# Numerators and projections joined into one step, and TensorE in program order in blocks 1 to 3, in a fused attention and two-layer expert kernel

## The chip, the cores and the metric

The kernel runs on one core of a Trainium2 chip. The metric is the device time of one execution in microseconds (us), as the median of three runs. Engines are named as in the profile: PE is TensorE (matmuls; PEld its weight loads), DVE is VectorE, ACT is ScalarE, POOL is GpSimd, SP is SyncE, which issues most transfers.

## The reference

Three stages follow each other. 2304 tokens are 4 batches of 576; there are 8 heads of 64.

```python
def phi(x):                                   # x: q or k
    proj = np.einsum('bhsd,df->bhsf', x, w_phi)          # 64 -> 128 features
    proj = proj - np.max(np.abs(proj), axis=-1, keepdims=True)
    return np.concatenate([np.exp(proj), np.exp(-proj)], axis=-1)
q_p, k_p = (phi(q), phi(k))
kv = np.einsum('bhsf,bhsd->bhfd', k_p, v)
z = np.sum(k_p, axis=2)
num = np.einsum('bhsf,bhfd->bhsd', q_p, kv)
den = np.einsum('bhsf,bhf->bhs', q_p, z)[..., None] + 1e-06
x = num / den                                 # heads side by side: 2304 x 512
# first layer, 512 -> 1536 -> 512
g = x @ w_gate
x2 = (g * (1.0 / (1.0 + np.exp(-g))) * (x @ w_val)) @ w_out
# second layer: one of 8 experts for each token, by argmax(x2 @ gate)
out[mask] = gate_w * eom * (np.maximum(x2[mask] @ w1[e], 0.0) @ w2[e])
```

## The kernel before

**Attention** is cut into 16 units, each two heads of one batch. Units 0 to 7 are computed in a first part whose order is a table (`PLAN_TABLE`, the same in both kernels). Units 8 to 15 are written as a list of steps (`steps`), and these are what the change touches. Unit u has these steps, each with its matmuls and what empties their PSUM banks:

- `step_kv`: the sums over k features and v (L350, L359), copied out by ACT;
- `step_tq`, three times: transposes of the projected q (L381), then two exponentials on ACT;
- `step_qk(u + 1, c)`, c = 0 to 2: a third of the next unit's projection of q and k (L310), 6 matmuls into a **pair** of banks. DVE then reads the pair twice, in `qk_sub`: the maximum (L318) and the subtraction (L321). ACT makes the exponentials;
- `step_num`: for each of the two heads the numerator and denominator (`num_mm`, L401, 20 matmuls into one bank), then `normalise` on DVE (L413 to L415);
- `step_tx`, twice: transposes of the result (L420), taken by ACT and DVE into `XH` and `XL`, the input of the first layer.

The matmuls of the first layer use the whole array. Those of `step_qk` use 64 of its rows, those of `step_kv` and `step_num` 64 of its columns. A fp32 matmul of the last two kinds stands as two in the trace: 6 are x12, 20 are x40.

**The first layer** works on 6 blocks of 384 tokens, each with 12 slices f. A slice has three runs of matmuls: gate (12, L538 to L540), value (12, the same lines), and the output of the slice before (9, L576 to L578). They own banks 0 to 4. The function `pace` is called after each run, 36 times per block, and spreads over them the steps of units 8 to 15; `need[n]` says up to which step block n has to come. After each of these calls (after two of three) `fill` runs one piece of the routing of the block before: `post_log` (4 transposes, L722), `post_mm` (L730), `route_a`, `route_b` (L764, L765).

**Banks 5, 6 and 7** are shared by all these steps and pieces. `bank_no` takes the one that was used longest ago, `pair_no` the pair of neighbours that was; in a tie the lowest number. Two pairs are possible, 5 and 6, or 6 and 7, so that two thirds of a projection in a row always share bank 6. Data dependencies, through banks too, become semaphore waits on the engine that comes later.

**Order.** After the first part a scheduler puts each engine's instructions in order, by the order of the program and by what it holds to be ready. An engine runs its instructions strictly in that order.

Of the kernel before, what the change touches and what calls it, by code (L numbers as in the profile page):

```python
# [24 lines left out]
NBLK, BT = 6, 384  # L25
# [4 lines left out]
QSW = 8  # L30
# [151 lines left out]
def kernel(ctx, tc, qT, kT, v1, wphi, w1cat, wlog, mw1, mw2, consts, out):  # L182
# [86 lines left out]
    state = {"n": 0, "banks": [0, 1, 2, 3, 4, 5, 6, 7], "rd": 0}  # L269
    used = {b: 0 for b in range(8)}  # L270
# [17 lines left out]
    def rot(key, lst):  # L288
        state[key] += 1
        return lst[state[key] % len(lst)]  # L290
# [4 lines left out]
    def load_qk(u):  # L295
        SP.dma_start(out=QK[u % 2][QROWS, :], in_=qT[u])
        SP.dma_start(out=QK[u % 2][KROWS, :], in_=kT[u])
# [4 lines left out]
    def two(u):  # L302
        return u % 2 if u < PROL else 0

    def qk_mm(u, c, b):

        for j in range(3):
            t0 = (3 * c + j) * P
            for rows, w in ((QROWS, 1), (KROWS, 0)):
                PE.matmul(PS[:, b + w, j * P:(j + 1) * P], QK[u % 2][rows, t0:t0 + P], wphi_sb[rows, :],  # L310
                          start=True, stop=True)
        if c == 2 and 8 < u < 14:
            load_qk(u + 2)

    def qk_sub(u, c, b):

        ps = PS[:, b:b + 2, :BT].rearrange("p w (j f) -> p w j f", f=P)
        DVE.tensor_reduce(out=MX, in_=ps, axis=AX.X, op=ALU.max, apply_absolute_value=True)  # L318
        t = KQ[two(u)][:, 3 * c:3 * c + 3, :].rearrange("p j (w f) -> p w j f", f=P)[:, 0:3:2]
        m = MX.rearrange("p w (j o) -> p w j o", o=1).to_broadcast([P, 2, 3, P])  # L320
        DVE.tensor_tensor(out=t, in0=ps, in1=m, op=ALU.subtract)  # L321

    def k_exp(u, c):
        kq, ts_ = KQ[two(u)], slice(3 * c, 3 * c + 3)
        t = kq[:, ts_, 0:P]
        ACT.activation(kq[:, ts_, P:2 * P], t, AF.Exp, scale=-1.0)
        ACT.activation(t, t, AF.Exp)
# [48 lines left out]
    def qp(u):  # L376
        return QP[two(u)] if u < QSW else QP[2]
# [15 lines left out]
    def num_mm(u, h, b):  # L393

        kv = KV[u % 2]
        ps = PS[:, b, :325].rearrange("p (s d) -> p s d", d=65)
        for i in range(5):
            for a in range(2):
                for g in HALVES:
                    t0 = h * S + i * P + (0 if i == 4 and h == 1 else g.start)  # L400
                    PE.matmul(ps[g, i, :], qp(u)[:, a, t0:t0 + 64], kv[:, a, h * 65:h * 65 + 65], start=(a == 0),  # L401
                              stop=(a == 1), skip_group_check=True)
# [7 lines left out]
    def normalise(h, b):  # L410
        ps = PS[:, b, :325].rearrange("p (s d) -> p s d", d=65)
        rd = rot("rd", RD)[:, :5].rearrange("p (s o) -> p s o", o=1)
        DVE.tensor_scalar(out=rd, in0=ps[:, :, 64:65], scalar1=1e-6, scalar2=None, op0=ALU.add)  # L413
        DVE.reciprocal(out=rd, in_=rd)
        DVE.tensor_tensor(out=XT[:, :, h * 64:h * 64 + 64], in0=ps[:, :, 0:64], in1=rd.to_broadcast([P, 5, 64]), op=ALU.mult)  # L415
# [31 lines left out]
    steps, mark = [], {}  # L447

    def add(f, *a):
        steps.append((f, a))  # L450

    def qk(u):
        return [(step_qk, u, c) for c in range(3)] if u < 16 else []

    def warmup(n):
        for _ in range(n):
            PE.matmul(PS[:, 4, :], warm[:, 0:P], warm, start=True, stop=True)

    add(step_ov)
    for u in range(QSW, 16):  # L460
        add(step_kv, u)
        for c in range(3):
            add(step_tq, u, c)
        x = qk(u + 1)
        for s_ in x[:2]:
            add(*s_)
        add(step_num, u)
        for s_ in x[2:]:
            add(*s_)
        add(step_tx, u, 0)  # L470
        add(step_tx, u, 1)
        mark[u] = len(steps)
    pos = [0]

    def run_to(n):
        while pos[0] < min(n, len(steps)):
            f, a = steps[pos[0]]
            f(*a)
            pos[0] += 1
# [46 lines left out]
    def split(i):  # L526
        if i < len(uses):
            split_hi(i)
            split_lo(i)
# [12 lines left out]
    def mm_gv(n, f, which):  # L542
        gv_mm(n, f, which)
        split(where[n, f, which] + 3)
# [16 lines left out]
    def act_g(n, f):  # L561
        g_tanh()
        g_mul()

    def act_v(n, f):
        v_mul()
        g_hi(f)
        g_lo(f)

    def o_mm(n, f):  # L570
        i = where[n, f, 2]
        woh, wol = WH[i % 4], WL[i % 4]
        for t in range(3):
            ps = PS[:, OUTB[t], :]
            ts_ = slice(t * P, (t + 1) * P)
            PE.matmul(ps, GH[f % 2][:, ts_], woh, start=(f == 0), stop=False)  # L576
            PE.matmul(ps, GH[f % 2][:, ts_], wol, start=False, stop=False)  # L577
            PE.matmul(ps, GL[f % 2][:, ts_], woh, start=False, stop=(f == NFT - 1))  # L578

    def mm_o(n, f):  # L580
        o_mm(n, f)
        split(where[n, f, 2] + 3)
# [128 lines left out]
    def post_x2(n, t):  # L711
        i = 3 * n + t
        x2 = X2[t]
        ACT.activation(x2, PS[:, OUTB[t], :], AF.Copy, scale=0.5)
        SP.dma_start(out=x2d[i * P:(i + 1) * P, 0:DM], in_=x2)
# [181 lines left out]
    def load_w(s, part):  # L897
        e = SP.value_load(EXI[0:1, s:s + 1], min_val=0, max_val=NE - 1)
        src = (mw1 if part == 0 else mw2)[ds(e, 1)].rearrange("o p c -> (o p) c")
        kw = {}  # L900
        if s >= 2:
            kw["cond"] = SP.value_load(CHI[0:1, s:s + 1], min_val=0, max_val=1)
        SP.dma_start(out=R[s % 2][:, part * 4096:(part + 1) * 4096], in_=src, **kw)
# [7 lines left out]
    def xt(s):  # L911
        ps = PS[:, XB, :]
        for k in range(4):
            PE.transpose(ps[:, k * P:(k + 1) * P], XG[s % 4][:, k * P:(k + 1) * P], ident)
        p3 = ps.rearrange("p (k t) -> p k t", k=4)
        ACT.activation(XCH[s % 2], p3, AF.Copy)  # L916
        tt(XCL[s % 2], p3, XCH[s % 2].bitcast(F32), ALU.subtract)
# [88 lines left out]
    POOL.memset(CHI[:, 0:2], 1)  # L1006
    first_part()
    state["banks"] = [5, 6, 7]
    need = {1: mark[8] - 2, 2: mark[11], 3: mark[15], 4: 0, 5: 0}
    prev = (0, NFT - 1)  # L1010

    def post(n):
        ops = []
        for t in range(3):
            ops += [(post_log, (n, t)), (post_mm, (n, t))]
        return ops + [(route_a, (n,)), (route_b, (n,))]
# [14 lines left out]
    def fill(n):  # L1031
        while todo and n > 0:
            f, a = todo.pop(0)
            f(*a)
            n -= 1

    todo = []
    for n in range(1, NBLK):
        s0, s1 = pos[0], max(need[n], pos[0])
        for f in range(NFT):  # L1040
            def pace(g):
                run_to(s0 + ((s1 - s0) * (3 * f + g) + 35) // 36)
                if g != 2 or n == 5:
                    fill(1)
            mm_gv(n, f, 0)
            act_g(n, f)
            pace(1)
            mm_gv(n, f, 1)
            act_v(n, f)
            pace(2)  # L1050
            if prev is not None:
                mm_o(*prev)
                if prev[1] == NFT - 1:
                    for t in range(3):
                        post_x2(prev[0], t)
                    todo += post(prev[0])
                    if prev[0] == 4:
                        todo += [(totals, (EARLY_T,)), (route_early, ()), (load_w, (0, 0)),
                                 (idle, ()), (idle, ()), (early, ())]
            prev = (n, f)  # L1060
            pace(3)
            if n == 5 and f == 10:
                xt(0)
            if n == 5 and f == 10:
                load_w(1, 0)
                load_w(1, 1)
    mm_o(*prev)
    for t in range(3):
        post_x2(5, t)
# [59 lines left out]
```

## Time and profile before

| | |
|---|---|
| time, median of 3 runs | 920.05 us (918.99 to 921.12) |
| the profiled execution | 920.25 us, its span 918.5 us |
| PE busy | 894.5 us, 97% of the span |
| DVE, ACT, POOL busy | 577.0, 559.4, 393.0 us |

The span falls into a first part (to about 170 us), blocks 1 to 3 with units 8 to 15 (to about 482 us), blocks 4 and 5 (to about 650 us), and the expert layer. Matmuls overlap in the trace, each being longer than the distance to the next, so that small gaps do not show in the busy time; the starts of neighbours show them.

### The profile page before, as it was taken

What the parts mean: (1) busy time and instruction counts of PE and PEld (TensorE: products, weight loads), DVE (VectorE), ACT (ScalarE), POOL (GpSimd) and SP (SyncE); (2) the same over time, 40 slices, a digit from 0 to 9 for tenths busy, and PEclk for the clock granted to TensorE, in tenths of its full rate; (3) what the DMA queues carried; (4) which work ended last, traced back from release to release, by engine and by line L of the source; (5) the groups of instructions that cost most, each with busy time, mean ns of one, the idle gap of its engine ahead of it and who ended that gap; (6) DMA issues with size and microseconds to landing.
All of it is one profiled execution on the core that took longest, in us unless ns stands there. A gap on an engine that the chain in (4) does not pass through costs nothing. (4 is left out here: it accounts for less than half of the span.)

```text
span 918.5 us, 18395 instructions
## 1 busy us (share of the span) xinstructions
PE 894.5 (97%) x7256; PEld 784.8 (85%) x7258; DVE 577.0 (63%) x977; ACT 559.4 (61%) x975; POOL 393.0 (43%) x318
## 2 busy tenths in 40 slices
PE   8899999999999999999999999979999999999995
PEld 6789989999998998898899999969877888888884
DVE  6999776443336435445433422772699988888993
ACT  5878775544353545544444444334688899888883
POOL 1667989445543434433345566566101111112200
PEclk9999999999999999999999999999999999999998
DMA  8767543200020111110000000090001147166240
GB/s 231 221 176 216 168 143 101 62 16 1 2 76 5 38 42 27 50 42 1 2 2 35 1 1 35 2 375 39 35 24 48 47 161 284 30 224 228 64 172 10
DMA packets 20940, 78.90 MB, mean 86 GB/s; under 512 B 5358, under 2 KB 5614, under 8 KB 19056
## 3 DMA queue, kind: packets, MB, share of 16 engines
q1 hardware_dynamic: 17280, 67.60, 22.8%
q0 software_dynamic: 3200, 9.48, 3.1%
q8 instruction: 59, 0.97, 0.4%
q10 hardware_dynamic: 368, 0.59, 0.3%
q14 instruction: 33, 0.27, 0.1%
HBM read 123.23 MB, written 10.00 MB: 145 GB/s over the span
## 5 line engine op out<-in xcount | busy, mean ns | idle before, releaser
L524 POOL TENSOR_TENSOR arena_r<-arena,arena_r 128x512 fp32r<-128x512 f32 x216 | 278.7, 1294 | 246.7 <-ACT arena_r L520 239.3
L520 ACT ACTIVATE arena_r<-arena 128x512 fp32r<-128x512 f32 x216 | 136.2, 631 | 229.3 <-PE banks L539 139.7
L538 PE MATMUL banks<-arena_r 128*128 128x384 f32 x576 | 202.4, 351 | 4.2 <-DVE arena L550 4.1
L890 DVE TENSOR_TENSOR arena_r<-arena,arena_r 128x1024 fp32r<-128x1024 f32 x160 | 193.1, 1255 | 20.3 <-ACT arena_r L889 18.9
L540 PE MATMUL banks<-arena_r 128*128 128x384 f32 x576 | 194.2, 337 | 0.0
L539 PE MATMUL banks<-arena_r 128*128 128x384 f32 x576 | 193.9, 337 | 0.0
L889 ACT ACTIVATE arena_r<-arena 128x1024 fp32r<-128x1024 f32 x160 | 161.9, 1067 | 18.4 <-PE banks L924 10.9
L550 DVE SCALAR_TENSOR_TENSOR arena<-arena,banks 128x384 f32<-128x384 f32 x72 | 39.7, 552 | 130.1 <-ACT arena L547 129.8
L924 PE MATMUL banks<-arena_r 128*128 128x512 f32 x480 | 117.0, 396 | 0.0
L538 PEld LDWEIGHTS banks<-arena_r 128*128 128x128 f32 x576 | 108.6, 189 | 9.5 <-DVE arena L550 4.9
L952 POOL DMA_INDIRECT out_dram<-arena x20 | 20.7, 1037 | 218.9 <-ACT arena L951 218.9
L539 PEld LDWEIGHTS banks<-arena_r 128*128 128x128 f32 x576 | 108.9, 189 | 1.2
L540 PEld LDWEIGHTS banks<-arena_r 128*128 128x128 f32 x576 | 108.7, 189 | 0.0
L924 PEld LDWEIGHTS banks<-arena_r 128*128 128x128 f32 x480 | 88.2, 188 | 20.3 <-ACT arena_r L916 2.1
L576 PE MATMUL banks<-arena_r 128*128 128x512 f32 x216 | 87.6, 405 | 0.0
L577 PE MATMUL banks<-arena_r 128*128 128x512 f32 x216 | 85.1, 394 | 1.0 <-POOL arena_r L524 1.0
L578 PE MATMUL banks<-arena_r 128*128 128x512 f32 x216 | 84.9, 394 | 0.0
L553 DVE TENSOR_TENSOR banks<-arena,banks 128x384 f32<-128x384 f32 x72 | 40.4, 561 | 44.8 <-PE banks L540 44.1
L946 PE MATMUL banks<-arena_r 128*128 128x512 f32 x160 | 62.7, 392 | 1.0 <-ACT arena_r L889 0.7
L948 PE MATMUL banks<-arena_r 128*128 128x512 f32 x160 | 62.4, 390 | 0.0
L947 PE MATMUL banks<-arena_r 128*128 128x512 f32 x160 | 62.4, 390 | 0.0
L318 DVE TENSOR_REDUCE arena<-banks 128x6 f32<-128x768 f32 x48 | 45.8, 954 | 23.6 <-PE banks L310 22.7
(119 smaller groups left out, 1327.2 us busy)
## 6 DMA issues: line engine op xcount, KB each, us to landing
arena<-mw SPq DMA_DIRECT2D x40, 2048.0 KB
ov_conv<-w1cat SPq DMA_DIRECT2D x24, 512.0 KB
arena<-w1cat SPq DMA_DIRECT2D x12, 512.0 KB
arena<-v SPq DMA_DIRECT2D x16, 325.0 KB
x2d<-arena SPq DMA_DIRECT2D x18, 256.0 KB
arena<-qT SPq DMA_DIRECT2D x15, 288.0 KB
arena<-kT SPq DMA_DIRECT2D x15, 288.0 KB
ov_gather<-x2d,arena POOLq DMA_INDIRECT x20, 4.3
```

What stands on the lines that cost most here:

```text
L520: ACT.activation(WH[i % 4], WR[f][w], AF.Copy)
L524: POOL.tensor_tensor(out=WL[i % 4], in0=WR[f][w], in1=WH[i % 4].bitcast(F32), op=ALU.subtract)
L538: PE.matmul(ps, wh[:, c], xh, start=(k == 0), stop=False)
L539: PE.matmul(ps, wh[:, c], xl, start=False, stop=False)
L540: PE.matmul(ps, wl[:, c], xh, start=False, stop=(k == 3))
L576: PE.matmul(ps, GH[f % 2][:, ts_], woh, start=(f == 0), stop=False)
L577: PE.matmul(ps, GH[f % 2][:, ts_], wol, start=False, stop=False)
L578: PE.matmul(ps, GL[f % 2][:, ts_], woh, start=False, stop=(f == NFT - 1))
L889: ACT.activation(h, src, AF.Copy)
L890: DVE.tensor_tensor(out=l, in0=src, in1=h.bitcast(F32), op=ALU.subtract)
L924: PE.matmul(PS[:, HB[h], :], lhs, w[:, h * 512:(h + 1) * 512], start=a, stop=b)
L946: PE.matmul(ps, HTH[:, k, :], wh[:, cs], start=(k == 0), stop=False)
```

## The change

Units 8 to 15 get another list of steps. The numerator of head h and third h of the next projection are one step, `step_num_qk(u, h)`, for h = 0 and 1: the 20 and the 6 matmuls stand behind each other, then `normalise`, then `qk_sub`. Its banks are written out: bank 7 and pair 5, 6 for h = 0; bank 5 and pair 6, 7 for h = 1. All three are marked as used at the same moment. The last third stays `step_qk(u + 1, 2)`. Three empty steps per unit take a call of `pace` each, and `step_tx` of unit u - 1 moves behind `step_tq` of unit u. The limits `need` move along: block 1 now ends after `step_tq` of unit 9, block 2 before `step_kv` of unit 13. Blocks 1 to 3 are recorded with PE in the order of the program; the scheduler still orders the other engines there, and all engines from block 4 on.

```diff
+    def step_num_qk(u, h):
+
+        b, pair = ((7, 5), (5, 6))[h]
+        state["n"] += 1
+        for x in (5, 6, 7):
+            used[x] = state["n"]
+        num_mm(u, h, b)
+        if u < 15:
+            qk_mm(u + 1, h, pair)
+        normalise(h, b)
+        if u < 15:
+            qk_sub(u + 1, h, pair)
+            k_exp(u + 1, h)
+
+    def step_idle():
+        pass
+
     add(step_ov)
     for u in range(QSW, 16):
+        mark["kv", u] = len(steps)
         add(step_kv, u)
         for c in range(3):
             add(step_tq, u, c)
-        x = qk(u + 1)
-        for s_ in x[:2]:
-            add(*s_)
-        add(step_num, u)
-        for s_ in x[2:]:
-            add(*s_)
-        add(step_tx, u, 0)
-        add(step_tx, u, 1)
-        mark[u] = len(steps)
+        mark["tx", u - 1] = len(steps)
+        if u > QSW:
+            add(step_tx, u - 1, 0)
+            add(step_tx, u - 1, 1)
+        add(step_idle)
+        add(step_num_qk, u, 0)
+        add(step_idle)
+        add(step_num_qk, u, 1)
+        if u < 15:
+            add(step_qk, u + 1, 2)
+        add(step_idle)
+    add(step_tx, 15, 0)
+    add(step_tx, 15, 1)
...
-    need = {1: mark[8] - 2, 2: mark[11], 3: mark[15], 4: 0, 5: 0}
+    need = {1: mark["tx", 8], 2: mark["kv", 13], 3: len(steps), 4: 0, 5: 0}
...
+    PE_ONLY = {mybir.EngineType.PE}
+    with tc.manual_schedule(engines=PE_ONLY):
+        for n in range(1, 4):
+            block(n)
+    for n in range(4, NBLK):
+        block(n)
```

Three places of PE's order follow, of before and of the changed kernel. In the latter, lines behind the new functions are 22 higher: L560 to L562 are gate and value, L598 to L600 the output, L744 `post_log`, L752 `post_mm`, L786 and L787 `route_b`.

Place A, PE, block 2: the first `post_log` of the routing of block 1. Before, it follows `step_kv` of unit 9:

```order
L577 MATMUL banks<-arena_r 128x512
L578 MATMUL banks<-arena_r 128x512
L350 MATMUL banks<-arena 64x130 x4
L359 MATMUL banks<-arena 64x65 x32
L722 MATMUL banks<-arena 128x128 x4
L538 MATMUL banks<-arena_r 128x384
L539 MATMUL banks<-arena_r 128x384
```

In the changed kernel it follows `step_num_qk(9, 0)`:

```order
L599 MATMUL banks<-arena_r 128x512
L600 MATMUL banks<-arena_r 128x512
L401 MATMUL banks<-arena,ov_qp 64x65 x20
L310 MATMUL banks<-arena 128x128 x6
L744 MATMUL banks<-arena 128x128 x4
L560 MATMUL banks<-arena_r 128x384
L561 MATMUL banks<-arena_r 128x384
```

The four transposes of the routing now stand directly behind a third of a projection, and the gate run behind them.

Place B, PE, block 2: the thirds 1 and 2 of the projection of unit 10. In the changed kernel `step_num_qk(9, 1)` and `step_qk(10, 2)` fall into one call of `pace` (there are 44 steps for 36 calls in this block):

```order
L561 MATMUL banks<-arena_r 128x384
L562 MATMUL banks<-arena_r 128x384
L401 MATMUL banks<-arena,ov_qp 64x65 x20
L310 MATMUL banks<-arena 128x128 x12
L598 MATMUL banks<-arena_r 128x512
L599 MATMUL banks<-arena_r 128x512
```

The two thirds, which were apart by at least one run of the first layer, are now one row of 12.

Place C, PE, block 2: `route_b` of block 1. Before, it follows a transpose of unit 9's result:

```order
L539 MATMUL banks<-arena_r 128x384
L540 MATMUL banks<-arena_r 128x384
L420 MATMUL banks<-arena 128x128 x2
L764 LDWEIGHTS arena
L764 MATMUL banks<-arena 128x8
L765 LDWEIGHTS arena
```

In the changed kernel it follows `step_num_qk(10, 0)`:

```order
L561 MATMUL banks<-arena_r 128x384
L562 MATMUL banks<-arena_r 128x384
L401 MATMUL banks<-arena,ov_qp 64x65 x20
L310 MATMUL banks<-arena 128x128 x6
L786 LDWEIGHTS arena
L786 MATMUL banks<-arena 128x8
L787 LDWEIGHTS arena
```

The six small matmuls of the ranks have the same neighbour as the transposes at place A. In block 3 `post_mm` (L752) stands in the same way behind `step_num_qk(13, 0)`.

## Rows read from the trace of the kernel before

**Rows 1.** Stretch, length; busy PE, PEld, DVE, ACT, POOL; clock; DMA share, GB/s.

```profile
170.00:482.00 312.00, 311.92 (x2956) 282.36 (x2955) 138.42 (x304) 146.42 (x311) 139.64 (x111) 1.00 0.10 27
```

**Rows 2.** Timeline of PE at 349 us (columns: start, length, engine, line, operation).

```profile
349.16 0.94 PE L310 MATMUL banks<-arena 64*128 64x128 f32 x12
350.03 0.44 PE L538 MATMUL banks<-arena_r 128*128 128x384 f32 x1
350.31 0.34 PE L539 MATMUL banks<-arena_r 128*128 128x384 f32 x1
350.48 0.35 PE L540 MATMUL banks<-arena_r 128*128 128x384 f32 x1
```

**Rows 3.** Timeline of PE at 355 us: both numerators in a row.

```profile
355.07 0.33 PE L539 MATMUL banks<-arena_r 128*128 128x384 f32 x1
355.25 0.34 PE L540 MATMUL banks<-arena_r 128*128 128x384 f32 x1
355.51 2.55 PE L401 MATMUL banks<-arena,ov_qp 128*64 128x65 f32 x80
358.00 0.50 PE L576 MATMUL banks<-arena_r 128*128 128x512 f32 x1
```

**Rows 4.** Timeline of PE in the first part: numerators directly ahead of a projection.

```profile
51.09 2.55 PE L401 MATMUL banks<-arena 128*64 128x65 f32 x80
53.57 0.94 PE L310 MATMUL banks<-arena 64*128 64x128 f32 x12
```

**Rows 5.** Timeline of PE in the first part: one numerator alone.

```profile
62.53 1.39 PE L401 MATMUL banks<-arena 128*64 128x65 f32 x40
63.84 0.55 PE L381 MATMUL banks<-arena 128*128 128x128 f32 x3
```

**Rows 6.** Waits of PEld from 170 to 490 us (columns: us in total, times, longest).

```profile
PEld banks L310 <- DVE arena L321: 0.8, 3, 0.3
```

**Rows 7.** Timeline of PE at 319 us.

```profile
318.91 1.25 PE L310 MATMUL banks<-arena 64*128 64x128 f32 x12
```

**Rows 8.** Timeline of PE and DVE at 417 us (in brackets: idle time before, and its end).

```profile
417.04 0.96 DVE L321 TENSOR_TENSOR arena<-banks,arena 128x768 f32<-128x768 f32 x1
417.26 1.72 PE L310 MATMUL banks<-arena 64*128 64x128 f32 x12
...
418.91 0.45 PE L538 MATMUL banks<-arena_r 128*128 128x384 f32 x1
419.02 0.96 DVE L318 TENSOR_REDUCE arena<-banks 128x6 f32<-128x768 f32 x1 [1.02 <-PE banks L310]
...
420.01 0.96 DVE L321 TENSOR_TENSOR arena<-banks,arena 128x768 f32<-128x768 f32 x1
```

**Rows 9.** Timeline of PE at 392 us: a routing piece directly behind a projection.

```profile
392.55 0.94 PE L310 MATMUL banks<-arena 64*128 64x128 f32 x12
393.42 0.65 PE L730 MATMUL banks<-arena 128*64 128x16 f32 x16
```

**Rows 10.** Timeline in the first part: PE waits for the subtraction of a projection.

```profile
8.59 0.96 DVE L321 TENSOR_TENSOR arena<-banks,arena 128x768 f32<-128x768 f32 x1
...
9.60 0.55 PE L381 MATMUL banks<-arena 128*128 128x128 f32 x3 [0.48 <-DVE arena L321]
```

**Rows 11.** Timeline of DVE at 390 us: one `normalise`.

```profile
389.99 0.17 DVE L413 TENSOR_SCALAR arena<-banks 128x5 f32<-128x5 f32 x1 [0.25 <-PE banks L401]
...
390.42 0.49 DVE L415 TENSOR_TENSOR arena<-banks,arena 128x320 f32<-128x320 f32 x1
```

**Rows 12.** Timeline at the end of block 0.

```profile
171.69 0.55 DVE L559 TENSOR_TENSOR arena_r<-banks,arena_r 128x384 fp32r<-128x384 f32 x1
...
171.89 0.39 PE L576 MATMUL banks<-arena_r 128*128 128x512 f32 x1
```

**Rows 13.** Timeline of PE in block 5, at 618 us.

```profile
617.82 0.56 PE L538 MATMUL banks<-arena_r 128*128 128x384 f32 x1 [3.13 <-DVE arena L550]
```

**Rows 14.** The four us after it: length, PE busy (matmuls), clock, DMA share, GB/s.

```profile
618.00:622.00 4.00, 4.00 (x15) 0.57 0.98 410
```

More of the change, by code (lines that the diff above doesn't have):

```diff
@@ L1037, with block @@
     todo = []
-    for n in range(1, NBLK):
+    def block(n):
+        nonlocal prev, todo
         s0, s1 = pos[0], max(need[n], pos[0])
```

## The prediction, made before the changed kernel was run

> **What bounds the kernel now.** I read the busy time by stretch first. From 170 to 482 us, where blocks 1 to 3 and units 8 to 15 run, PE is busy 311.92 of 312 us, DVE 138.42, ACT 146.42, POOL 139.64 [rows 1]. PE sets the end of this stretch, and the change touches no other. But a busy PE can hide gaps of some tenths, because a matmul is longer (0.34 us) than the distance to the next (0.17) [rows 2]. So the second view is PE's timeline, from start to start. There the same run of matmuls takes the same time wherever it stands, to a few ns, with two exceptions, both a third of a projection (L310): 1.25 and 1.72 us long [rows 7, 8], where the usual one is 0.94 [rows 2]. They cost 0.31 + 0.78 = 1.09 us together. The list of waits names their end: L310 waits for DVE's L321, the subtraction of the third before [rows 6]. The reader is to see in it that PE has almost no waits to lose in this stretch: 1.1 us of 312. What the change can give is that, and the price of switching PE between full and half arrays. What it can cost is every new wait of PE, in full.
>
> **The switches.** Going from a full-array run into a half-array one costs about 0.09 us: 355.25 to 355.51 is 0.26 where full runs go on at 0.17 [rows 3]. Coming back costs about 0.11 on the first matmul of the full run: 350.03 to 350.31 is 0.28 instead of 0.17 [rows 2]. So a step that needs no entry and return of its own saves 0.20. In PE's two orders between 170 and 480 us I count 41 entries from a full-array run before and 36 after: -5 x 0.20 = -1.0 us. Against that, both numerators in a row take 2.49 (355.51 to 358.00) [rows 3], one alone 1.31 (62.53 to 63.84) [rows 5]: two halves cost 2.62, +0.13 for each of 8 units, +1.0 us. The joint from a numerator to a projection is no saving: 51.09 to 53.57 is 2.48, as long as with a return to the full array [rows 4, 3]. Sum of the switches: 0.0, and I keep ±0.5 for it.
>
> The page TensorEngine Tiling (Array Packing) of the Trainium skill, Key Properties, says that a change of the tiling mode, not of the tile alone, drains the engine. It speaks against this change, since a numerator (64 columns) and a projection (64 rows) are two modes; the 2.48 us agree. Without that drain, about what a return costs, 0.11, would fall away at the 14 joints: an estimate of 1.5 us less.
>
> **The new waits.** `step_num_qk` marks banks 5, 6 and 7 as used at one moment, so whatever asks for a bank next gets bank 5. After h = 0 this is half of the pair that the projection has just filled. It comes free when DVE has read the pair twice. With PE in program order nothing can be put ahead of the step that waits: the gate run behind it and everything behind that stand still.
>
> The price of such a wait is in the trace. The projection of 417 us ends at 417.26 + 1.72 = 418.98; DVE starts L318 at 419.02 and ends L321 at 420.01 + 0.96 = 420.97 [rows 8]. PE follows 0.05 behind: 8.59 + 0.96 = 9.55, matmul at 9.60 [rows 10]. So a step that needs the bank starts at 421.02, where the next matmul did start at 418.91. One wait is 2.11 us. The lower bound is DVE's two passes alone, 1.92; the upper 2.11 plus one other instruction of DVE in front, about 0.55 as L559 [rows 12], 2.66. I take 2.11, since `normalise` (389.99 to 390.91, 0.92) [rows 11] has about the projection's own 0.87 on PE to run in.
>
> The order of the changed kernel has four steps that come directly behind a projection whose banks they need:
> - block 2, `post_log` behind `step_num_qk(9, 0)` (place A);
> - block 2, third 2 of unit 10 behind third 1 in the same call (place B): pairs 5, 6 and 6, 7 share bank 6;
> - block 2, `route_b` behind `step_num_qk(10, 0)` (place C);
> - block 3, `post_mm` behind `step_num_qk(13, 0)`.
>
> Before, a routing piece behind a projection found the third bank free: L730 starts 0.87 behind the start of L310, no wait [rows 9]. So four times 2.11 = +8.44 us. At place B, DVE still has the second head's numbers and a copy of the routing in front: +0.2 (0 to 0.55).
>
> Smaller ones. In block 3 a `post_log` stands behind `step_num_qk(13, 1)`; there bank 5 holds the numerator, and only `normalise` is left: +0.1 (0 to 0.4). At the end of block 0 the value run of block 1 now stands ahead of the first third of the last output run, and its bank is read by L559 until 171.69 + 0.55 = 172.24, while PE is ready at 171.89 [rows 12]: +0.4. The restart of PE after a wait is not shown by itself; the nearest row is the 0.11 of a return to the full array [rows 2], so 0 to 0.15 each, taken as 4 x 0.08 = +0.3 (0 to 0.6).
>
> The old waits of 1.09 came at pairs of thirds with one run of 2.1 us between: six such pairs, two of which waited. The changed order has four (units 11, 12, 13 and 15's last thirds), with `normalise` besides: 4/6 x 1.09 = +0.7 (0 to 1.3), and -1.09 for the old ones.
>
> **Moved steps that cost nothing.** `step_tx` runs later by about five steps, but its results are first read by block 3 (units 8 to 11) and by blocks 4 and 5; all stand ahead of that in PE's order, the last as before one output run ahead of block 4. On SP the stores of the first layer's output change places with the loads of q, k and v; these are issued a whole unit, over 25 us, ahead of their use. On POOL one weight split changes places with four memsets. DVE, ACT and POOL are busy less than half of the stretch [rows 1]. Were that cover gone, one late load would show as a PE wait for a DMA. From block 4 on, all engines keep their order, so a delay of PE passes whole to the end.
>
> **Sum.** 8.44 + 0.2 + 0.1 + 0.4 + 0.3 + 0.7 - 1.09 + 0.0 = +9.05 us. The profiled execution took 920.25 (span 918.5 and 1.75 around it), so 929.3; it lies 0.2 above the median of 920.05, so I forecast 929.1, 1.0% slower. With all the low bounds: 4 x 1.92 + 0.4 - 1.09 - 0.5 = +6.5, 926.5. With all the high ones: 8.44 + 4 x 0.55 + 0.4 + 0.4 + 0.6 + 1.3 - 1.09 + 0.5 = +12.8, 932.8.
>
> **The rivals.**
> 1. *The clock falls at the waits.* In block 5 PE stood 3.13 us and came back at the lower of its two levels, 1.2 GHz instead of 2.4: clock 0.57 over the next four us, 15 matmuls [rows 13, 14]. At 0.174 each, 23 would have fitted, so a fall costs 8 x 0.174 = 1.4 us. If all four waits of 2.1 us did this, 929.1 + 5.6 = 934.7; one of them, 930.5. For it: they are the longest gaps of the stretch. Against: they are a third shorter than 3.13, and the two gaps of 0.3 and 0.8 in the stretch left the clock at 1.00 [rows 1, 7, 8]. The page TensorE: Matmul & The Clock Gate, Loop structure matters more than you think, warns of this case, matmul bursts with waits between; rows 13 and 14 agree for the longer gap, none shows one of 2 us. Chance 0.10.
> 2. *DVE comes later than I think.* At each of the four places the instructions of gate and value, 0.55 each, or the routing's could stand ahead of L318 and L321, two or three of them: 4 x 1.4 = 5.6 more, 934.7. Against: DVE is busy 44% of the stretch. Chance 0.06.
> 3. *Not slower: the waits are covered.* If one run of the first layer (12 x 0.174 = 2.1 us) stood between a projection and the next user of its banks in all cases, DVE's two passes would be hidden; that is the point from which it decides. Then 0.4 + 0.3 + 0.7 - 1.09 = +0.3 is left, 920.4, or 919 with the joints cheaper than I take them. For it: most of the projections in the new order do have such a run behind them. Against: at the four places it stands behind the waiting step, and PE does not pass it. Chance 0.05.
> 4. *The change does little:* the scheduler's order is kept in effect, 920. The orders at places A to C say otherwise. Chance 0.02.
>
> **How the numbers follow.** The forecast has 0.77. The range of 926.5 to 933.0 spans its bounds and single falls of the clock, and leaves out the rest of rivals 1 and 2, and 3 and 4, under 0.2. A measurement of this kernel can tell about 0.2%, 1.8 us, from no change: faster 0.02, from rival 3; same 0.05, from rivals 3 and 4; slower 0.93.
>
> **What would show it.** Right: in PE's timeline of blocks 1 to 3 four gaps of about 2 us, ended by L321, in front of `post_log`, `post_mm`, `route_b` and one L310 of place B; block 3 ends some 9 us later, and the rest is shifted by that; the clock stays at 1.00 until block 5. Wrong: less than two such gaps (rival 3); a clock below 1.00 between 170 and 500 us (rival 1); gaps of 3 us and more at full clock (rival 2); a changed length of blocks 4 and 5 or of the expert layer, which I hold to be untouched.

## The result, and the profile after

| | before | after |
|---|---|---|
| time, median | 919.52 us (918.58 to 921.12, 4 runs) | 930.61 us (928.26 to 932.32, 4 runs) |
| the profiled execution, its span | 920.25, 918.5 us | 930.35, 928.6 us |
| PE busy | 894.5 us, 97% | 896.8 us, 97% |
| last output matmul of block 0 starts at | 175.85 us | 175.84 us |
| last output matmul of block 4 starts at | 569.32 us | 580.66 us |
| last matmul of all ends at | 908.09 us | 919.02 us |

The changed kernel is 1.012 times as long as the kernel before (interval 1.0105 to 1.0135): 1.2% slower, 11.1 us by the medians. The forecast was 929.1, with a range of 926.5 to 933.0.

Between the last output matmuls of blocks 0 and 4 lie 393.47 us before and 404.82 us after, +11.35 us. I call this **the stretch** from here on. Behind it the kernels are alike (338.77 and 338.36 us to the end of the last matmul). The page of the profile hides all of this: PE's share is 97% in both. It stands in PE's list of waits between 170 and 500 us (columns: what waits and for what; us in total, times, longest). In the kernel before this list is empty; the 0.8 us of [rows 6] are waits of PEld. After:

```profile
PE banks L310 <- DVE arena L321: 2.3, 1, 2.3
PE banks L744 <- DVE arena L321: 2.1, 1, 2.1
PE banks L752 <- DVE arena L321: 2.1, 1, 2.1
PE banks L786 <- DVE arena L321: 2.1, 1, 2.1
PE banks L560 <- DVE arena_r L581: 0.2, 1, 0.2
PE banks L744 <- DVE arena L415: 0.2, 1, 0.2
```

Four waits for the subtraction of a projection (L321) are there, each once, ahead of `post_log` (L744), the second third at place B (L310), `route_b` (L786) and `post_mm` (L752). One of them in full, from the timelines of PE and DVE at place A (start, length, engine, line; in brackets the idle time before, and its end):

```profile
270.29 0.94 PE L310 MATMUL banks<-arena 64*128 64x128 f32 x12
270.40 0.17 DVE L413 TENSOR_SCALAR arena<-banks 128x5 f32<-128x5 f32 x1 [1.73 <-PE banks L401]
...
270.82 0.49 DVE L415 TENSOR_TENSOR arena<-banks,arena 128x320 f32<-128x320 f32 x1
271.27 0.96 DVE L318 TENSOR_REDUCE arena<-banks 128x6 f32<-128x768 f32 x1
272.26 0.96 DVE L321 TENSOR_TENSOR arena<-banks,arena 128x768 f32<-128x768 f32 x1
273.37 0.63 PE L744 MATMUL banks<-arena 128*128 128x128 f32 x4 [2.14 <-DVE arena L321]
273.75 0.42 PE L560 MATMUL banks<-arena_r 128*128 128x384 f32 x1
```

`normalise` (L413 to L415) ends at 271.31, just behind the projection, which ends at 271.23. DVE's two passes follow it, and PE starts 0.15 us behind the second, 2.14 us after its last matmul had ended. The gate run (L560) stands behind the waiting transposes and starts at 273.75; it needs nothing of them, and experiment 4 starts it right behind the projection.

The second reading is the clock. Four us behind places A and B, and 3.4 us beginning about 1 us behind place C and 2 us behind the wait of `post_mm`; the first row covers the times of [rows 1] (from and to, length; busy PE, PEld, DVE, ACT, POOL; clock; DMA share, GB/s):

```profile
170.00:482.00 312.00, 303.07 (x2836) 274.26 (x2836) 135.42 (x293) 143.54 (x303) 131.95 (x103) 0.99 0.10 27
273.40:277.40 4.00, 4.00 (x36) 3.72 (x37) 1.20 (x3) 1.91 (x4) 0.66 (x1) 1.00 0.02 4
283.40:287.40 4.00, 3.98 (x28) 3.43 (x29) 2.22 (x3) 1.72 (x4) 0.00 (x0) 1.00 0.46 112
312.90:316.30 3.40, 3.40 (x28) 2.96 (x29) 1.38 (x4) 0.97 (x2) 0.49 (x1) 0.50 0.00 0
411.90:415.30 3.40, 3.40 (x12) 3.01 (x11) 0.94 (x2) 1.12 (x2) 1.04 (x1) 0.50 0.00 0
```

Behind two of the four waits TensorE runs at its lower level (1.2 GHz, 0.50 of the higher one) for 3.4 us. At half the pace that would be 1.7 us lost each time; runs 5 and 6 measure 1.5. In PE's timeline the fall can be seen as it comes, 1.1 us after the wait's end at place C; the distance from start to start goes from 0.17 to 0.32 us while no engine is waited for:

```profile
311.78 0.17 PE L786 MATMUL banks<-arena 128*128 128x8 bf16 x1 [2.07 <-DVE arena L321]
...
312.54 0.34 PE L560 MATMUL banks<-arena_r 128*128 128x384 f32 x1
312.71 0.37 PE L561 MATMUL banks<-arena_r 128*128 128x384 f32 x1
312.88 0.52 PE L562 MATMUL banks<-arena_r 128*128 128x384 f32 x1
313.20 0.52 PE L560 MATMUL banks<-arena_r 128*128 128x384 f32 x1
```

Before, no fall stood in this stretch [rows 1]; the one of block 5 [rows 13, 14] is there in both kernels (at 618.0 and 630.3 us).

### The profile page after: what moved, and what is told of

Same layout as the page of the kernel before. It is cut to its first block, busy times and chain, and to the rows that moved or that the text cites. A ratio compares the mean times of both kernels' runs of the same rounds, so it can differ in the third digit from the quotient of the medians.

```text
span 928.6 us, 18402 instructions
## 1 busy us (share of the span) xinstructions
PE 896.8 (97%) x7258; PEld 787.1 (85%) x7258; DVE 578.5 (62%) x977; ACT 560.3 (60%) x975; POOL 392.5 (42%) x318
## 5 line engine op out<-in xcount | busy, mean ns | idle before, releaser
L560 PE MATMUL banks<-arena_r 128*128 128x384 f32 x576 | 202.7, 352 | 4.3 <-DVE arena L572 4.1
L562 PE MATMUL banks<-arena_r 128*128 128x384 f32 x576 | 195.2, 339 | 0.0
L560 PEld LDWEIGHTS banks<-arena_r 128*128 128x128 f32 x576 | 109.1, 189 | 9.4 <-DVE arena L572 4.9
L562 PEld LDWEIGHTS banks<-arena_r 128*128 128x128 f32 x576 | 109.1, 189 | 0.0
L598 PE MATMUL banks<-arena_r 128*128 128x512 f32 x216 | 87.5, 405 | 0.0
L600 PE MATMUL banks<-arena_r 128*128 128x512 f32 x216 | 85.2, 396 | 0.0
L581 DVE TENSOR_TENSOR arena_r<-banks,arena_r 128x384 fp32r<-128x384 f32 x72 | 40.0, 555 | 31.2 <-ACT arena_r L578 31.1
```

Of the source, the lines that this page charges most:

```text
L560: PE.matmul(ps, wh[:, c], xh, start=(k == 0), stop=False)
L562: PE.matmul(ps, wl[:, c], xh, start=False, stop=(k == 3))
```

## The experiments

Two questions. Does a wait need both halves of the change, the marks that give away the pair's bank next and the program order that lets nothing pass? And do the falls come from the waits? The stretch is read in each experiment's profiled execution from PE's timeline; times are medians, ratios against runs of the kernel before on the same chip.

| kernel | time, us | ratio (interval) | the stretch, us | against before |
|---|---|---|---|---|
| before | 919.33 to 919.75 | 1 | 393.47 | |
| after | 930.61 | 1.012 (1.0105 to 1.0135) | 404.82 | +11.35 |
| 1, numerator's bank given away first | 925.0 | 1.0053 (1.0038 to 1.0068) | 398.94 | +5.47 |
| 2, and thirds 1 and 2 apart | 922.3 | 1.0032 (1.0019 to 1.0045) | 396.63 | +3.16 |
| 3, old steps, PE in program order | 919.31 | 1.0001 (0.999 to 1.0012) | 393.46 | -0.01 |
| 4, new steps, scheduler's order | 921.88 | 1.0031 (1.0019 to 1.0042) | 396.42 | +2.95 |
| 5, waits 1 us longer | 938.24 | 1.0208 (1.0193 to 1.0224) | 411.82 | +18.35 |
| 6, waits filled with matmuls | 927.69 | 1.0097 (1.0081 to 1.0113) | 401.76 | +8.29 |
| 7, before, gap of block 5 filled | 917.8 | 0.9978 (0.9969 to 0.9988) | 393.51 | +0.04 |
| 8, rearranged steps | 919.43 | 1.0 (0.9989 to 1.001) | 393.74 | +0.27 |

**1. The numerator's bank is given away first.** The order of PE and the steps are the change's.

```diff
         for x in (5, 6, 7):
             used[x] = state["n"]
+        used[b] -= 0.5
```

> The changed kernel, but step_num_qk marks the numerator's bank as used longest ago, so that the next one to ask gets that bank and not half of the projection's pair. Theory (the four gaps are waits for a bank that the subtraction L321 still reads): the gaps in front of post_log, route_b and post_mm fall from 2.1 to about 0.2 us, what is left of normalise; the one of place B stays at 2.4. 3 x 1.9 = 5.7 us less, and without the falls of the clock behind route_b and post_mm (about 1.6 each in the profiled run) up to 3.3 more: 921.5 to 925. Rival (PE would wait anyway, since DVE comes late to everything there): unchanged, 930.

Measured: 925.0 us (922.98 to 925.19, 4 runs), at the upper end of what was expected. Three of the four long waits are gone; what follows a joined step takes the numerator's bank and waits for `normalise` (L415) alone. PE's list of waits between 170 and 500 us:

```profile
PE banks L310 <- DVE arena L321: 3.5, 2, 2.3
PE banks L745 <- DVE arena L415: 0.4, 2, 0.2
...
PE banks L753 <- DVE arena L415: 0.2, 1, 0.2
PE banks L787 <- DVE arena L415: 0.2, 1, 0.2
```

The 3.5 us are the wait of place B, 2.3, which the mark can't help since two thirds in a row share bank 6, and a new one of 1.25 at 318 us, where a third comes one output run behind the joined step and now gets a bank of its pair. A fall stands behind B this time (at 282.4 us, clock 0.50). So the marks make three of the four waits. Most of the 5.47 us that are left are place B's wait and the fall behind it, and the new wait.

**2. Thirds 1 and 2 apart as well.** As 1, with one of the empty steps put between them.

```diff
         add(step_num_qk, u, 1)
+        add(step_idle)
         if u < 15:
             add(step_qk, u + 1, 2)
-        add(step_idle)
```

> As e1_bank, and the last third of the projection changes places with the empty step behind it, so that it no longer falls into the call of the second third. Theory: the last of the four gaps goes too, 2.4 us less than e1_bank and no fall of the clock before block 5: 919.5 to 921.5, the time of the kernel before. New small waits of step_kv for the exponentials of the last third, which now comes closer to it, 0.1 to 0.2 each. Rival (joined steps cost PE time of their own): 923 or more with no gap over 0.5 us.

Measured: 922.3 us (5 runs), 0.8 above what was expected. No wait for L321 is left and no fall in the stretch, but `step_kv` now comes so soon behind the last third that PE waits for the exponentials of ACT, up to 1.0 us where 0.1 to 0.2 was expected:

```profile
PE banks L359 <- ACT arena L327: 1.0, 1, 1.0
PE banks L745 <- DVE arena L415: 0.2, 1, 0.2
...
PE banks L753 <- DVE arena L415: 0.2, 1, 0.2
PE banks L787 <- DVE arena L415: 0.2, 1, 0.2
```

Most of these waits are too short for the list and show from start to start. The second matmuls of `step_kv` (L359) take 1.97 us up to their neighbour in the kernel before (1.87 once); here they take 2.13 to 2.24 us in five of the eight units, and 3.19 in one. One unit in both kernels (timelines of PE, the kernel before first; the next line starts at 372.69 and at 383.93):

```profile
370.73 2.04 PE L359 MATMUL banks<-arena 128*64 128x65 f32 x64
381.70 2.30 PE L359 MATMUL banks<-arena 128*64 128x65 f32 x64
```

All of `step_kv` takes 2.45 us more than before, so this is most of the 3.16 us. The rest is in small pieces, and I did not settle it.

**3. Program order alone.** The steps of the kernel before; PE in program order in blocks 1 to 3.

```diff
-    for n in range(1, NBLK):
+    def block(n):
+        nonlocal prev, todo
...
+    PE_ONLY = {mybir.EngineType.PE}
+    with tc.manual_schedule(engines=PE_ONLY):
+        for n in range(1, 4):
+            block(n)
+    for n in range(4, NBLK):
+        block(n)
```

> The kernel before with its own steps, and PE in program order in blocks 1 to 3: the one half of the change. Theory (program order hurts only where a step asks for a bank that is still read, which the old steps do not do): +0.4 at the end of block 0, and the old waits about as before: 919.5 to 921. Rival (program order is the cause by itself): 925 and more.

Measured: 919.31 us (12 runs), the kernel before within 0.12%. PE's whole list between 170 and 500 us:

```profile
PE banks L310 <- DVE arena L321: 0.3, 1, 0.3
PE banks L538 <- DVE arena_r L559: 0.2, 1, 0.2
```

The order of the program costs nothing where no step asks for a bank that is not free.

**4. The new steps alone.** The change without the program order: `for n in range(1, NBLK): block(n)`, the scheduler orders PE.

> The changed kernel with its steps and banks, but PE ordered by the scheduler in all blocks: the other half. There the scheduler has put a gate run between the projection and post_log, route_b and post_mm, and cut the thirds at place B into pieces. Theory (a wait needs both halves: the marks that give away the pair's bank, and an order that lets nothing pass): gaps of at most 0.5 us, 919.5 to 921.5. Rival (the steps and their banks are the cause by themselves): 926 and more.

Measured: 921.88 us (6 runs), a little above what was expected. None of the four long waits is there. What the scheduler did at place A (timeline of PE):

```profile
269.45 0.94 PE L310 MATMUL banks<-arena 64*128 64x128 f32 x12
270.31 0.44 PE L560 MATMUL banks<-arena_r 128*128 128x384 f32 x1
...
272.68 0.60 PE L744 MATMUL banks<-arena 128*128 128x128 f32 x4
273.04 0.42 PE L561 MATMUL banks<-arena_r 128*128 128x384 f32 x1
...
278.57 0.93 PE L310 MATMUL banks<-arena 64*128 64x128 f32 x6 [0.41 <-DVE arena L415]
279.43 0.50 PE L598 MATMUL banks<-arena_r 128*128 128x512 f32 x1
```

It put 13 matmuls of gate and value between the projection and the transposes (270.31 to 272.68, 2.4 us), which is more than the 2.14 us of the wait and covers it. At place B it cut the second third in two, and it cut two other thirds as well. Pieces of runs cost switches: between 170 and 500 us its timeline changes 80 times between the full array, numerators or sums, and projections, the kernel before and the changed one 74 times. From start to start the projections take 21.37 us of the stretch, against 19.33 before, where the old waits of 1.09 are in them: the cut thirds and their waits are 2.0 of the 2.95 us. The rest is in small pieces.

By runs 1 to 4, each half alone costs 0 and 2.95 us of the stretch, both together 11.35: a wait of 2 us needs, here, a bank that is not free and an order that lets nothing pass.

**5. Longer waits.** The changed kernel, with one more reduction on DVE ahead of the two passes at the four places.

```diff
+        if (u, h) in ((9, 0), (10, 0), (13, 0), (9, 1)):
+            DVE.tensor_reduce(out=MX, in_=PS[:, pair:pair + 2, :BT].rearrange("p w (j f) -> p w j f", f=P), axis=AX.X,
+                              op=ALU.max, apply_absolute_value=True)
```

> The changed kernel, with one more reduction on DVE (0.96 us, its result is not used) ahead of the two passes over the pair in the four steps behind which PE waits, so that each of the four gaps grows from 2.1 to about 3.1 us. Theory A, the clock falls because of the gap, and a longer one brings it down more surely: the four waits give 4 x 0.96 = +3.8 us, and with falls of about 1.65 us at all four places instead of two another +3.3, so about 937.5 us. Theory B, the falls have another cause than the gaps: the same two, +3.8 alone, about 934.4 us. Below 933 the gap would not grow by what is added to DVE, and the wait would not be DVE's.

Measured: 938.24 us (937.92 to 938.36, 4 runs), as theory A has it. The waits are 1.0 us longer, and 3.4 us at the lower level follow each of the four (same columns as above):

```profile
PE banks L310 <- DVE arena L321: 3.3, 1, 3.3
PE banks L747 <- DVE arena L321: 3.1, 1, 3.1
PE banks L755 <- DVE arena L321: 3.1, 1, 3.1
PE banks L789 <- DVE arena L321: 3.1, 1, 3.1
```

```profile
275.30:278.70 3.40, 3.40 (x13) 3.40 (x13) 0.69 (x1) 0.79 (x2) 0.00 (x0) 0.50 0.02 5
288.90:292.30 3.40, 3.40 (x9) 2.56 (x9) 1.79 (x2) 0.00 (x0) 0.00 (x0) 0.50 0.65 167
319.60:323.00 3.40, 3.40 (x23) 2.96 (x24) 1.53 (x5) 0.80 (x3) 0.19 (x1) 0.51 0.02 5
418.60:422.00 3.40, 3.40 (x11) 3.40 (x12) 0.16 (x1) 0.35 (x1) 0.00 (x0) 0.50 0.00 0
```

The stretch is 7.00 us longer than in the changed kernel: 4 x 1.0 of waiting, which leaves 3.0 for two more falls, 1.5 each. The mean clock over the span is 0.986 to 0.988 in all four executions; in the changed kernel's it is 0.990 to 0.993.

**6. The waits filled.** The changed kernel, with ten matmuls of no use behind the projection at the four places. PE waits for the same banks, but works meanwhile.

```diff
+        if (u, h) in ((9, 0), (10, 0), (13, 0), (9, 1)):
+            xs = XH[:, 0 if u == 13 else 2, 0, :]
+            for _ in range(10):
+                PE.matmul(PS[:, GB, :BT], xs[:, 0:P], xs, start=True, stop=True)
```

> The changed kernel, with ten matmuls of 384 columns over the full array behind the projection at the four places where PE waits; their result is not used, and they take about 10 x 0.174 = 1.7 us of each gap of 2.1 us. PE is then busy while it waits for DVE, and everything behind starts when it did. Theory A, the falls of the clock come from PE standing still: clock 1.00 in blocks 1 to 3, and the two falls of the profiled execution (+3.3 us) go, about 927.3 us, with the four waits still paid in full. Theory B, the falls have another cause: about 930.6 us, with falls near 313 and 412 us as in the changed kernel. Above 931 the ten matmuls would not fit into the gap.

Measured: 927.69 us (926.22 to 928.63, 4 runs), as theory A has it. At place A (timeline of PE), and the whole of blocks 1 to 3 (same columns as above):

```profile
271.55 2.01 PE L471 MATMUL banks<-arena_r 128*128 128x384 f32 x10
273.76 0.63 PE L748 MATMUL banks<-arena 128*128 128x128 f32 x4 [0.21 <-DVE arena L321]
```

```profile
170.00:500.00 330.00, 328.87 (x3046) 297.66 (x3045) 143.43 (x312) 152.99 (x323) 144.63 (x115) 1.00 0.09 26
```

No fall is left, and the stretch is 3.06 us shorter than in the changed kernel, with forty matmuls more. Each wait takes the same time from start to start as in the changed kernel (place A: 270.68 to 273.76 here, 270.29 to 273.37 there), so the difference is the falls alone. The mean clocks of the four executions are 0.995 to 0.997, none as low as the changed kernel's. So the falls come from PE standing still at the four places, and in the profiled execution they made 3.06 of the 11.35 us. The other 8.29 are the waits with the small terms.

**7. The gap of block 5 filled.** The kernel before, with 18 matmuls of no use ahead of the gate run of [rows 13].

```diff
+            if (n, f) == (5, 7):
+                b = bank_no()
+                xs = XH[:, 2, 0, :]
+                for _ in range(18):
+                    PE.matmul(PS[:, b, :BT], xs[:, 0:P], xs, start=True, stop=True)
             mm_gv(n, f, 0)
```

> The kernel before, with 18 matmuls of 384 columns over the full array (result not used) in the 3.5 us in which PE stands still in block 5 ahead of a gate run, about 18 x 0.174 = 3.1 us of it. The change under study is not in it. Theory A, gaps bring the clock down in some executions, in this place too, and this is what spreads the times of the kernel before (917.2 to 920.6 us, longer with a lower clock): without the fall, which costs 1.4 us, the median goes from 919.5 to about 918.1 and the clock of the runs is higher. Theory B, the fall has another cause: 919.5, with the fall near 618 us still there. Above 920 the matmuls would not fit into the gap.

Measured: 917.8 us (12 runs) against 919.75 of the kernel before: 0.22% faster, the one version here that beats both. PE's timeline, and the four us from the gate run on, to be set beside [rows 14] (columns as above):

```profile
615.74 3.31 PE L1049 MATMUL banks<-arena_r 128*128 128x384 f32 x18
619.09 0.44 PE L538 MATMUL banks<-arena_r 128*128 128x384 f32 x1
```

```profile
619.09:623.09 4.00, 4.00 (x23) 4.00 (x24) 1.68 (x3) 2.02 (x4) 2.27 (x2) 1.00 1.00 419
```

These four us hold 23 matmuls instead of 15, and block 5 takes 82.55 us instead of 84.15 (from the last output matmul of block 4 to its own). The mean clock is 0.996 or 0.997 in all 12 executions; in the kernel before it lies between 0.993 and 0.997, and the longer executions are mostly those with the lower clock. So the cause holds in a place that the change does not touch.

**8. Rearranged steps.** The mark of 1; an empty step behind each of the two joined steps, ahead of the next third; `step_tx` at the end of its unit, as before; the scheduler's order.

```diff
...
-        mark["tx", u - 1] = len(steps)
-        if u > QSW:
-            add(step_tx, u - 1, 0)
-            add(step_tx, u - 1, 1)
-        add(step_idle)
         add(step_num_qk, u, 0)
         add(step_idle)
         add(step_num_qk, u, 1)
+        add(step_idle)
         if u < 15:
             add(step_qk, u + 1, 2)
-        add(step_idle)
+        mark["tx", u] = len(steps)
+        add(step_tx, u, 0)
+        add(step_tx, u, 1)
+        mark["end", u] = len(steps)
...
-    need = {1: mark["tx", 8], 2: mark["kv", 13], 3: len(steps), 4: 0, 5: 0}
+    need = {1: mark["tx", 8], 2: mark["end", 11], 3: len(steps), 4: 0, 5: 0}
```

> A version meant to lose nothing: joined steps, with the numerator's bank marked as the one to give away first, an empty step behind the first two joined steps, each ahead of the next third of the projection, the transposes of a unit's result again at the end of the unit, 12 full units' steps placed as the calls allow, and PE ordered by the scheduler in all blocks. If the waits are all that the change cost, none is left and it takes the time of the kernel before, 919.5 us, up to 921; if the joined steps themselves cost something (about 2.5 us were left with the scheduler's order and the change's own list of steps), about 922. Faster than 918 is not expected of either, since the switches of the array sum to about nothing.

Measured: 919.43 us (12 runs), the time of the kernel before within 0.11%. Its waits of PE in the stretch are three of 0.2 us for `normalise`. So the joined steps are neither a loss nor a gain in themselves. What the change lost lies in their places, their marks and PE's order; this run alters all three and doesn't tell them apart.

## Why the prediction was right, and where it was not

**The four waits** came where the prediction put them, of the size that it gave them: idle 2.14, 2.27, 2.07 and 2.07 us, 8.55 in all, against 8.44 and 0.2 for place B. From start to start the four lost 8.92 us over the usual distance, 0.37 more, where the sum had 0.3 for a restart. That term was right in size and not in its reason: run 6, where PE is busy during the waits, takes the same time from start to start. The 0.37 are mostly the overlap of neighbours, which a wait takes away: a third is 0.94 us long, its distance to the next matmul 0.87 [rows 2]. The price had come from one row of DVE's two passes [rows 8] and held to 2% at all four places, with the 0.2 added at B. Its reason at B was half right: ahead of `normalise` stood no copy of the routing but a subtraction of the first layer (L581, 280.13 to 280.69), and `normalise` started at 280.60.

**The old waits** (1.09 us) are gone, as forecast, and **the switches** are nothing: 11.35 less 8.92, less 0.22 for the `post_log` that waits for `normalise` (forecast 0.1), less 3.1 to 3.4 for the falls, plus 1.09, leaves +0.2 to -0.1. Run 4 shows both sides of that sum: the numerators take 21.05 us instead of 19.76, gate and value 208.99 instead of 210.03. The page TensorEngine Tiling (Array Packing) of the Trainium skill, Key Properties, says that a change of the mode drains the engine. The trace agrees: a numerator takes 1.31 us up to a projection (278.90 to 280.21 at place B), as much as up to the full array [rows 5]; had the 14 joints cost no drain, an estimate of 1.5 us would be missing here.

**The step that failed is the place of the clock.** It stood as rival 1 with a chance of 0.10 instead of in the sum, and a clock below 1.00 between 170 and 500 us was one of the prediction's own signs of being wrong. The argument against it was that 2.1 us is a third shorter than the gap of 3.13 us in block 5, and that the gaps of 0.3 and 0.8 us left the clock alone. But no row between 0.8 and 3.13 bore on it; a cost that no row shows should have been bounded between none and four falls, with one or two taken. Run 6 showed it as 3.06 us in the profiled execution. The price of one fall, 1.4, was near: 1.5 by runs 5 and 6, 1.6 by run 7. The page TensorE: Matmul & The Clock Gate of the Trainium skill, Loop structure matters more than you think, which was named beside that rival, sets matmuls back to back, which stay warm, against matmuls with long waits between them, which run cold. Runs 5 to 7 agree.

**A term that was too large:** pairs of thirds with one run between, +0.7. They cost nothing that shows: the list has no wait for L321 but the four, and the four last thirds (at 320.16, 351.17, 382.18 and 457.55 us) take 0.87 us up to their neighbour, as any other. I had carried over the rate at which such pairs waited before, two of six, instead of reading DVE at each. Run 1 shows that such a pair can wait, 1.25 us, when the marks hand out the banks in another turn.

**A term that fell away:** the 0.4 at the end of block 0. The gap is there (0.57 us instead of 0.17 between two starts, at 171.2; 0.2 of idle time in the list), but block 0 ends at the same time in both kernels, 175.84 and 175.85, because PE had come to it 0.5 us earlier. The end of block 0 lies between 174.98 and 177.08 us in the profiled executions here, so 0.4 can't be read from it.

So the forecast, 1.5 us under the median, was right in the mechanism and the places of the waits. That it came so near is in part luck, since its misses have both signs: falls +3.1, pairs -0.7, the end of block 0 -0.4, and the kernel before at 919.52 here instead of 920.05. Of the profiled executions' difference, 10.10 us, the stretch has 11.35; the part behind it to the end of the last matmul is 0.41 shorter, and what follows the last matmul about 0.8 shorter.

**Rival 2** (DVE later) did not occur in its size: at place A nothing of DVE but `normalise` stands ahead of the two passes, and the one instruction more at place B cost 0.2 us. **Rival 3** (the waits are covered) is what run 4 does at place A, with program order taken away. **Rival 4** (little changes) is out by the four waits.

## What to carry to other kernels

A wait is made of two things, a buffer that is not free and an order in which nothing can pass the one who waits for it; look for both before pricing a change of either. Where an order is fixed by hand, say of each step whose bank it takes and what reads that bank last; where several buffers are marked as used together, give away first the one whose reader is done first. And a wait of TensorE, where it sets the end, costs its length and perhaps the clock behind it: price both.

## What the hardware showed that I had not expected

- Waits of 2.07 us brought the clock down in one profiled execution, while waits of 2.14 and 2.27 us in the same execution did not; in run 6, PE stood still for 3.15 us in block 5 and the clock over the four us behind it was 1.00 (row below). So in a single execution the length alone does not decide. It changes how often: waits of 3.1 and 3.3 us did it at all four places of run 5.

```profile
626.27 0.44 PE L564 MATMUL banks<-arena_r 128*128 128x384 f32 x1 [3.15 <-DVE arena L576]
```

```profile
626.20:630.20 4.00, 3.93 (x23) 3.93 (x24) 1.69 (x4) 2.02 (x4) 2.19 (x2) 1.00 1.03 430
```

- The fall does not come with the wait but up to 2 us behind it (place C: wait over at 311.78, slower from 312.9; `post_mm`: over at 410.03, slower from 411.9). A matmul that is slow for no visible reason can have its cause earlier in the timeline.
- Matmuls whose result nobody uses can make a kernel faster: 18 of them, in time that PE would have stood still anyway, were worth 1.95 us in run 7.
